# Talking-heads attention and an FFT mixer on one core: a batch's rows in seven blocks of 60 and one of 40 places

## The chip, the core and the metric

One core of a Trainium2 chip runs the whole program. The metric is the device time of one execution in microseconds; the time of a kernel is the median of its runs. A profile is of one further execution, whose own time is given beside it.

## The reference

For 8 batches, 12 heads, 448 places and 64 elements a head: scores of all heads, mixed over the heads, softmax, mixed over the heads again, times v; then an FFT over places and channels, a layer norm, and a two-layer network with a ReLU.

```python
scores = scale * np.matmul(q, k.transpose(0, 1, 3, 2))
scores = np.einsum('bhij,hg->bgij', scores, w_pre)
attn = softmax(scores)
x = matmul(np.einsum('bhij,hg->bgij', attn, w_post), v)   # to (8, 448, 768)
u = x + np.real(np.fft.fft(np.fft.fft(x, axis=1), axis=2))
un = (u - mean(u)) / np.sqrt(var(u) + 1e-06)
out = u + np.maximum(un @ w_ch1, 0.0) @ w_ch2
```

All is float32.

## The kernel before

The program has two stages. The mixing stage (`mix_phase`) makes u for each batch and stores it in DRAM; the feed-forward stage (`ffn_phase`) loads u in 512-row tiles, normalises it and multiplies by the weights with a Strassen-like scheme of seven products. The stages meet in one place: the first tiles of u are loaded when the mixing stage has given its memory back, and the last Fourier pieces of the last batch run as "parts" between the first products.

**Steps.** The mixing stage goes through places in steps of 20: a step holds five places on each of four quarters (two row blocks of PSUM's partitions z, two tiles x), each with 12 heads, 60 rows in all. A batch is 24 steps (`GS`), the stage 192 (`TOT`). For a step T:

- four gathers (`emit_gather`, line 475, on SP's queue) bring rows of scores from a block's tile Sb into Kr, so that heads lie on partitions; they are issued four steps ahead (`LG`);
- premix (`emit_premix`, line 486, PE, 8 matmuls) mixes heads, two steps (`LM`) before the step's postmix; two maxima on DVE (line 493), two exponentials on ACT (line 500), reciprocals on DVE (507, 508) and two scalings on POOL (510);
- postmix (`emit_postmix`, line 520, PE, 8 matmuls) mixes again, and DVE transposes the result into Pv (`emit_turn`, line 531).

**Blocks.** Three steps (`BS`) share a block of 60 places: `emit_qk` (line 459) computes the scores of a block in three shares of 8 matmuls, one for each pair of heads; ACT copies them to Sb (the helper at line 330). Sb has two buffers.

**Groups.** Two blocks make a group of six steps (`GT`), 112 rows of x (`GR`). A batch has four groups. When its steps are over, `emit_av` (line 547) multiplies Pv by v in three calls of 28 instructions, 120 columns wide, and ACT copies the result to XT, in an order of places that lets groups be added as mirror images: `PLACE` says where a group's two blocks go and which columns are set to zero (line 569). Neighbouring groups need a few rows twice, so 8 blocks of 60 places compute 480 places for 448 rows. `emit_x` (line 580) transposes XT into X; there are six buffers of X and one of XT.

**Fourier part.** The two X of a pair are folded on POOL (`fold`, lines 601 to 622), z is computed from them (`emit_z`, line 645), and `emit_s2` (line 661) adds the second transform into X by four DVE additions (lines 672, 674). After the second of a pair, X is stored: one X by SP (line 692), the other by an indirect DMA on POOL (line 684), and for the second pair a single row by SP (line 690).

**Order.** [...] A loop over steps s goes through one of two orders of pieces (`ORDERS`, for even and odd s). Pieces beside the steps stand in lists with a due step counted from the batch's first: `AT_T` (transpositions of q and k, line 434), `AT_L` and `AT_V` (loads on POOL's queue), `AT_QK`, `AT_AV`, `AT_X`, `AT_Z`, `AT_S`. Copies out of PSUM wait in a list `pend` until a `flush`; stores wait in `later` until the scale of a following step, folds go two to a step. The loop ends 29 steps after the first step of the last batch (`AT_X[-1]`):

```python
while s <= TOT - GS + AT_X[-1]:
    ...
return fold_rest, [lambda t, fn=fn: part(fn, t)
                   for _, _, fn in fill["full"] + [(0, 0, None)]]
```

Pieces of kind "full" that are due later are the parts. The feed-forward stage loads tiles 0 and 1 of u (line 910, SP), takes statistics (935), computes powers on POOL (940 to 943), runs the folds that are left (`fold_rest`, POOL), normalises (951) and transposes (960). In the products of the first tile (`first`, line 1026) a part is run after the first product and after the fourth to the seventh, and one after each of the second layer's (line 1099). The conversion of the weights from 64-bit floats (lines 231 to 267) goes on DVE, one operation a step, and later in the feed-forward stage.

Of the kernel before, what the change touches and what calls it, by code (L numbers as in the profile page):

```python
# [10 lines left out]
F32 = mybir.dt.float32  # L11
# [18 lines left out]
R = 5  # L30
KR = R * NH
RS = 12
NB = 56
BS = 3
GT = 2 * BS
GR = 2 * NB
NG = S // GR
GS = NG * GT
ROWS = ((0, NB), (S - GR + 1, S - NB + 1), (GR, GR + NB), (GR * 2 + 1, GR * 2 + 1 + NB))
PR = (GR, GR + 1)  # L40
PN = GR + 1


PLACE = ((0, 1, (GR,)), (GR - 1, -1, (0, GR)), (GR, -1, ()), (1, 1, (0,)))
XW = GR + 12

ENDS = (GR, GR * 2 + 1, GR * 3 + 1, S)
TOT = B * GS
# [10 lines left out]

SH = S // 2
DH = DM // 2
DQ = DH // 2
CW = DQ // 2 + 1
# [8 lines left out]

AT_T = ((6, 10), (17, 18), (14, 16))
AT_L = ((-4, -3), (-2, -1), (0, 1), (2, 8), (12, 13), (14, 15))
AT_V = ((3, 4), (5, 6), (7, 7))
AT_QK = ((1, 2, 2), (0, 1, 2), (0, 1, 2), (1, 1, 2),  # L80
         (0, 1, 2), (0, 1, 2), (0, 1, 2), (0, 1, 2))
AT_AV = ((1, 2, 3), (0, 1, 5), (3, 4, 5), (1, 2, 4))
AT_X = (11, 20, 24, 29)
AT_Z = (39, 39, 41, 41)
AT_S = ((40, 44), (48, 54))

ORDERS = tuple(o.split() for o in (
    "conv pre post flush AV max0 exp0 "
# [202 lines left out]
def mix_phase(ctx, tc, rest, ident, q, k, v, w_pre, w_post, u_scr, u_rev, wts):  # L291
# [8 lines left out]
    def pool(name, bufs=1, **kw):  # L300
        return ctx.enter_context(tc.tile_pool(name=name, bufs=bufs, **kw))

    def late(name, bufs=1):
        return rest.enter_context(tc.tile_pool(name=name, bufs=bufs, side="right"))
# [8 lines left out]
    wts.open(ctx, tc)  # L313
    pvv = pool("pvv")
    ppv = pool("ppv", 2)
    pxt = pool("pxt")
    pxx = late("pxx", 6)
    pxs = late("pxs")
    pxf = late("pxf")
    pzz = late("pzz")  # L320
# [63 lines left out]
    batches = [dict() for _ in range(B)]  # L384
    first = {}
    START = sorted(range(3), key=lambda xx: max(AT_T[xx]))
    blocks = [dict(b=n // (2 * NG), r0=ROWS[n // 2 % NG][n % 2]) for n in range(2 * NG * B)]
    groups = [dict(b=n // NG, gi=n % NG) for n in range(NG * B)]
    steps = [dict() for _ in range(TOT)]

    def emit_load_qk(b, xx, nm, y):
# [54 lines left out]
    def emit_qk(n, xx):  # L446

        bk = blocks[n]
        st = batches[bk["b"]]
        if "Sb" not in bk:  # L450
            bk["Sb"] = psb.tile([P, 6, S], F32, name="Sb", tag="Sb")
        r0 = bk["r0"]
        pss = [ms_tile() for _ in range(2)]
        for y in range(2):
            for lo in (r0 + MG * y, r0 + MG * y + 32):
                o = 64 * y + lo - r0 - MG * y
                hi = min(lo + 32, r0 + 64)
                for x in range(2):
                    nc.tensor.matmul(  # L459
                        pss[x][o:o + hi - lo, :S],  # L460
                        st["qT", xx][64 * x:64 * x + 64, y, lo:hi],
                        st["kT", xx][64 * x:64 * x + 64, y, :],
                        start=True, stop=True)
        return [lambda x=x: copy(ENG["QK"][x], bk["Sb"][:124, 2 * xx + x, :],
                                 pss[x][:124, :S]) for x in range(2)]

    def emit_gather(T):

        Kr = pkr.tile([P, 2, S], F32, name="Kr", tag="Kr")
        Sb = blocks[T // BS]["Sb"]  # L470
        row = _row(Sb)
        for z in range(2):
            for x in range(2):
                p0 = MG + 4 * (T % BS) + 2 * z + x
                nc.sync.dma_start(
                    out=Kr[64 * x:64 * x + KR, z, :],
                    in_=_ap(Sb, p0 * row, [[RS * row, 2 * R], [S, 6], [1, S]]))
        steps[T]["Kr"] = Kr

    def emit_premix(T):  # L480
# [44 lines left out]

    def emit_turn(T):

        g = groups[T // GT]
        if T % GT == 0:
            g["Pv"] = ppv.tile([P, GT, 2 * S], F32, name="Pv", tag="Pv")  # L530
        nc.vector.transpose(  # L531
            g["Pv"][:, T % GT, :].rearrange("p (z s) -> p z s", z=2),
            steps[T]["po"][:, :, :S])
        steps[T].clear()

    def emit_av(g, pr):

        st = batches[g["b"]]
        Pv = g["Pv"]
        rp = _row(Pv)  # L540
        nu = GT * 4
        pss = [ms_tile() for _ in range(2)]
        for jb in range(C7):
            for x in range(2):
                for y in range(2):
                    i = 2 * pr + x
                    nc.tensor.matmul(  # L547
                        pss[y][64 * x:64 * x + 64, :nu * R],
                        st["v", pr][64 * y:64 * y + 64, x, jb * D:(jb + 1) * D],
                        _ap(Pv, 64 * y * rp + 32 * jb + R * i,  # L550
                            [[rp, 64], [HS, nu], [1, R]]),
                        start=(jb == 0), stop=(jb == C7 - 1))
        if pr == 0:
            g["XT"] = pxt.tile([P, 6, XW], F32, name="XT", tag="XT")
        XT = g["XT"]
        rx = _row(XT)
        first, sg, none = PLACE[g["gi"]]

        def done(y):
            rs = _row(pss[y])  # L560
            for e in range(2):

                o = MG + first + sg * NB * e
                dst = _ap(XT, (3 * y + pr) * XW + o, [[rx, P], [sg * RS, R], [sg, RS]])
                src = _ap(pss[y], 60 * e, [[rs, P], [1, R], [R, RS]])
                copy(ENG["AV"][y], dst, src)
            if y == 1 and pr == 2:
                for o in none:
                    nc.vector.memset(XT[:, :, MG + o:MG + o + 1], 0.0)
        return [lambda y=y: done(y) for y in range(2)]  # L570

    def emit_x(g):
        X = pxx.tile([PN, DM], F32, name="X", tag="X")
        XT = g.pop("XT")
        g["X"] = X
        evs = []
        for u in range(2):
            ps = ms_tile()
            for i in range(3):
                nc.tensor.transpose(ps[:PN, i * P:(i + 1) * P],  # L580
                                    XT[:, 3 * u + i, MG:MG + PN], ident[:, :])
            evs.append(lambda u=u, ps=ps: copy(ENG["X"][u], X[:, u * DH:(u + 1) * DH],
                                               ps[:PN, :DH]))
        if g["gi"] % 2:
            fold(g)
        return evs

    def fold(g):
# [1 line left out]

        st = batches[g["b"]]
        pair = g["gi"] // 2
        Xa, Xb = groups[g["b"] * NG + g["gi"] - 1]["X"], g["X"]
        pl = nc.gpsimd
        box = []

# [103 lines left out]
    def due(kind, at, fn):  # L700
        fill[kind].append((at, len(fill[kind]), fn))
# [4 lines left out]
    for b in range(B):  # L706
# [23 lines left out]
        for pr in range(3 if b else 0):  # L730
            for y in range(2):
                due("none", f + AT_V[pr][y], lambda b=b, pr=pr, y=y: emit_load_v(b, pr, y))
        for n in range(0 if b else 2, 2 * NG):
            for xx in range(3):
                due("QK", f + BS * n - 7 + AT_QK[n][xx],
                    lambda n=2 * NG * b + n, xx=xx: (emit_qk(n, xx), n))
        for n in range(NG):
            g = groups[b * NG + n]
            for pr in range(3):
                due("AV", f + GT * (n + 1) + AT_AV[n][pr],  # L740
                    lambda g=g, pr=pr: (emit_av(g, pr), None))
            due("full", f + AT_X[n], lambda g=g: emit_x(g))
        for n, at in enumerate(AT_Z):
            due("full", f + at, lambda b=b, n=n: emit_z(b, n // 2, n % 2))
        for pair in range(2):
# [27 lines left out]
    s = int(min(v_[0][0] for v_ in fill.values()))  # L773
    ET = mybir.EngineType
    with tc.manual_schedule(engines={ET.PE, ET.DVE, ET.Activation, ET.Pool}):
        while s <= TOT - GS + AT_X[-1]:
            old = len(later)
            n = take("none", s)
            ahead, now = 0 <= s + LM < TOT, 0 <= s < TOT
            for op in ORDERS[s % 2]:  # L780
                if op == "flush":
                    flush()
                elif op in fill:
                    take(op, s)
                elif op == "conv":
                    if s >= 4:
                        wts.deal(1)
                elif op == "gather":
                    if 0 <= s + LG < TOT:
                        if any(e[2] is not None and e[2] <= (s + LG) // BS for e in pend):  # L790
                            flush()
                        emit_gather(s + LG)
                elif op == "scale":
                    if ahead:
                        emit_scale(s + LM)
                    for _ in range(old):
                        later.pop(0)()

                    if s < TOT - 3:
                        for _ in range(min(len(folds), 1 if n and s > 3 else 2)):  # L800
                            folds.pop(0)()
                elif op in ("post", "turn"):
                    if now:
                        (emit_postmix if op == "post" else emit_turn)(s)
                elif ahead:
                    (emit_premix if op == "pre" else emit_max if op[0] == "m"
                     else emit_exp)(s + LM, *map(int, op[3:]))
            s += 1
        flush()
        wts.deal(1000)  # L810
# [559 lines left out]
```

## Time and profile before

| | us |
|---|---|
| median of 3 runs | 2387.02 |
| lowest, highest | 2384.95, 2389.32 |
| the profiled execution | 2384.91 |
| its span | 2383.1 |
| PE busy | 2307.2 (97%) |
| DVE busy | 1739.4 (73%) |
| POOL busy | 1145.6 (48%) |
| ACT busy | 1131.5 (47%) |

The span is the stretch from the first to the last instruction in the profile; the execution's own time is 1.8 us longer. A row of the profile names a line of the code, an engine, the tiles (out<-in), and how often the instruction ran. The trace counts a float32 matmul of the small shapes twice, so that the 8 instructions of a premix are x16 there. "Kr<-Sb" is a gather, "ms" a PSUM tile of the pieces beside the steps, "mx" and "po" those of premix and postmix.

### The profile page before, as it was taken

How to read it: one execution, taken by the hardware profiler on the slowest of the kernel's cores; microseconds unless marked ns; L12 is line 12 of the kernel's file. 1: busy time of each engine (PE TensorE's matmuls, PEld its weight loads, DVE VectorE, ACT ScalarE, POOL GpSimd, SP SyncE). 2: the span in 40 equal slices, each digit the busy share in tenths (PEclk: the TensorE clock that was granted, in tenths of full speed). 3: DMA queues.
4: the chain of work that ended last, by engine and by line, in shares of the span. 5: the costliest groups of instructions: out<-in, count | busy, mean ns of one | idle time of the engine just before them, and what ended most of it. 6: DMA issues, size and time to landing. Idle time of an engine off the chain costs nothing.

```text
span 2383.1 us, 59994 instructions
## 1 busy us (share of the span) xinstructions
PE 2307.2 (97%) x22856; PEld 1740.8 (73%) x22856; DVE 1739.4 (73%) x3636; ACT 1131.5 (47%) x3101; POOL 1145.6 (48%) x1684
## 2 busy tenths in 40 slices
PE   6999999999999969999999999999999999999998
PEld 2555555555565557767777779999899999999997
DVE  3888888889887746776676767777767777776556
ACT  4777776666667522232122224444444444444444
POOL 3687877878776451211234353334333433343333
PEclk8999999999999979999999999999999999999999
DMA  7565555656554555656888795569456846674553
GB/s 169 167 175 169 183 170 159 198 163 182 174 174 156 196 161 174 222 194 228 243 246 226 209 310 127 153 174 260 126 152 179 227 133 184 166 214 118 146 127 67
DMA packets 215627, 429.07 MB, mean 180 GB/s; under 512 B 39086, under 2 KB 137670, under 8 KB 215342
## 3 DMA queue, kind: packets, MB, share of 16 engines
q1 hardware_dynamic: 144686, 283.82, 34.8%
q0 software_dynamic: 64656, 139.45, 26.8%
q8 instruction: 183, 3.00, 0.6%
q10 hardware_dynamic: 6000, 1.97, 0.5%
q14 instruction: 102, 0.84, 0.1%
HBM read 213.16 MB, written 129.39 MB: 144 GB/s over the span
## 4 chain that ended last, share of the span: by engine, by line
PE 85%; DMA 4%; DVE 4%; POOL 2%; issue 2%; ACT 1%; SPq 1%; ACTq 0%; POOLq 0%; DVEq 0%
PE psP L1026 17%; PE psP L1156 10%; PE psR L1026 9%; PE mx L486 7%; PE ms L547 6%; PE psP L1099 6%; PE ms L459 5%; PE po L520 5%; PE psR L1156 5%; PE psQ L1026 4%; PE psR L1099 3%; DMA Kr<-Sb 3%; PE psQ L1156 2%; PE ms L661 2%; PE psQ L1099 1%
## 5 line engine op out<-in xcount | busy, mean ns | idle before, releaser
L1026 PE MATMUL psP<-ub,w1t 128*128 128x256 f32 x2016 | 482.8, 380 | 0.2 <-DVE h L1045 0.2
L1026 PEld LDWEIGHTS psP<-ub,w1t 128*128 128x128 f32 x2016 | 380.7, 191 | 49.1 <-DVE h L1045 0.6
L510 POOL TENSOR_SCALAR PP<-PP,rcp 128x448 f32<-128x448 f32 x384 | 254.7, 672 | 220.6 <-DVE rcp L508 190.2
L500 ACT ACTIVATE PP<-mx,nmx 128x448 f32<-128x448 f32 x384 | 240.7, 632 | 167.4 <-DVE nmx L493 153.5
L493 DVE TENSOR_REDUCE nmx<-mx 128x1 f32<-128x448 f32 x384 | 222.6, 617 | 91.0 <-PE mx L486 89.5
L1190 POOL DMA_DIRECT2D out_dram<-od x109 | 133.1, 1405 | 280.8 <-DVE od L1187 147.6
L486 PE MATMUL mx<-Kr,kw 60*32 60x448 f32 x3072 | 233.8, 549 | 15.9 <-DMA Kr<-Sb 12.2
L990 POOL TENSOR_TENSOR hq<-h 128x256 f32<-128x256 f32 (+1 forms) x168 | 104.3, 621 | 293.4 <-ACT h L1046 173.2
L1026 PE MATMUL psR<-ub,w1t 128*128 128x256 f32 x1008 | 231.3, 379 | 0.0
L1187 DVE TENSOR_TENSOR od<-od 128x768 f32<-128x768 f32 x196 | 188.6, 974 | 52.4 <-ACT od L1184 50.6
L531 DVE STREAM_TRANSPOSE Pv<-po 128x896 f32<-128x896 f32 x192 | 212.6, 1107 | 10.4 <-PE po L520 7.3
L520 PE MATMUL po<-PP,kw 60*32 60x448 f32 x3072 | 212.3, 537 | 2.7 <-POOL PP L510 1.8
L459 PE MATMUL ms<-kT,qT 64*32 64x448 f32 (+1 forms) x3072 | 205.6, 544 | 7.2 <-ACT qT L330 6.3
L1026 PEld LDWEIGHTS psR<-ub,w1t 128*128 128x128 f32 x1008 | 191.4, 190 | 25.9
L330 ACT COPY Sb<-ms 124x448 f32<-124x448 f32 x384 | 184.0, 542 | 33.0 <-DMA Kr<-Sb 15.1
L547 PEld LDWEIGHTS ms<-Pv,vv 64*64 64x64 f32 x5376 | 143.1, 132 | 70.9 <-issue 36.0
L1184 ACT COPY od<-psP 128x192 f32<-128x192 f32 x390 | 125.0, 320 | 145.6 <-PE psP L1156 141.4
L213 POOL DMA_DIRECT2D raw<-in_moe_w_ch_dram x88 | 53.0, 603 | 261.9 <-DVE tmp L257 255.1
L547 PE MATMUL ms<-Pv,vv 64*64 64x120 f32 x5376 | 166.7, 267 | 1.1 <-issue 1.1
L1099 PE MATMUL psP<-w2t,h 128*128 128x384 f32 x448 | 153.7, 486 | 0.0
L1045 DVE TENSOR_TENSOR h<-h,psP 128x512 f32<-128x512 f32 x42 | 28.8, 687 | 148.9 <-PE psP L1026 148.7
L459 PEld LDWEIGHTS ms<-kT,qT 64*32 64x32 f32 (+1 forms) x3072 | 67.9, 106 | 79.9 <-issue 51.8
(141 smaller groups left out, 4602.1 us busy)
## 6 DMA issues: line engine op xcount, KB each, us to landing
ub<-ub SPq DMA_DIRECT2D x294, 384.0 KB
Kr<-Sb SPq DMA_DIRECT2D x768, 105.0 KB
out_dram<-od POOLq DMA_DIRECT2D x137, 384.0 KB, 6.1
w1t<-w SPq DMA_DIRECT2D x42, 384.0 KB
w2t<-w SPq DMA_DIRECT2D x42, 384.0 KB
raw<-in_moe_w_ch_dram POOLq DMA_DIRECT2D x56, 256.0 KB, 5.2
raw<-in_moe_w_ch_dram POOLq DMA_DIRECT2D x32, 384.0 KB, 4.0
w<-wst POOLq DMA_DIRECT2D x92, 128.0 KB, 3.9
```

Of the source, the lines that this page charges most:

```text
L459: nc.tensor.matmul(pss[x][o:o + hi - lo, :S], st["qT", xx][64 * x:64 * x + 64, y, lo:hi], st["kT", xx][64 * x:64 * x + 64, y, :], start=Tr ...
L486: nc.tensor.matmul(mx[x][64 * z + o:64 * z + o + 32, :S], kw1[64 * x:64 * x + KR, o:o + 32], Kr[64 * x:64 * x + KR, z, :], start=True, sto ...
L493: nc.vector.tensor_reduce(nmx[:, :], steps[T]["mx"][x][:, :S], axis=AX.X, op=ALU.max, negate=True)
L500: nc.scalar.activation(steps[T]["PP"][:, x, :], steps[T]["mx"][x][:, :S], ACTF.Exp, bias=steps[T]["nmx", x][:, :], accum_out=steps[T]["den ...
L510: nc.gpsimd.tensor_scalar(PP[:, x, :], PP[:, x, :], rcp[:, x:x + 1], 1.0, op0=ALU.mult, op1=ALU.mult)
L520: nc.tensor.matmul(po[o:o + 32, z, :S], kw2[64 * z:64 * z + KR, y, :], PP[64 * z:64 * z + KR, :, c * HS:(c + 1) * HS], start=True, stop=True)
L531: nc.vector.transpose(g["Pv"][:, T % GT, :].rearrange("p (z s) -> p z s", z=2), steps[T]["po"][:, :, :S])
L547: nc.tensor.matmul(pss[y][64 * x:64 * x + 64, :nu * R], st["v", pr][64 * y:64 * y + 64, x, jb * D:(jb + 1) * D], _ap(Pv, 64 * y * rp + 32 ...
L1026: nc.tensor.matmul(p[:, m, :], w1[i][:, kc, m * P:(m + 1) * P], ub[:, kc, :], start=i in (0, 4, 1)[:3 - seed] and m == kc == 0, stop=kc == ...
L1099: nc.tensor.matmul(p, h[:, LHS[i], kf, x * P:(x + 1) * P], w2[i][:, kf, :], start=i in (0, 4, 1)[:3 - (c > 0)] and kf == 0, stop=kf == FM ...
L1156: nc.tensor.matmul(ps[j, key][:, :DQ], a, b, start=m in (0, 4), stop=True, skip_group_check=True)
L1187: eng.tensor_tensor(D[j][:, :, :], D[j][:, :, :], D[k][:, :, :], op=ALU.add)
```

## The change

A batch has 23 steps. Its 448 rows lie in eight blocks, seven of 60 places and one of 40 (`BLOCKS`: first place, places of a fifth, steps, group, first column, direction). Blocks lie without overlap in the two halves of the batch; the block of 40 has two steps, so that the third and fourth blocks make five steps (`GROUP_AT`), and the width of the products with v is 120 or 100 columns. Two blocks no longer make one group's rows exactly: a block that straddles two groups is written to one XT, and the columns that belong to the other are copied over on POOL (`SPILL`). For this XT has two buffers, and X five. Since the second group of a pair can be ready before the first, `emit_x` runs in the order 0, 1, 3, 2 (`AT_X`), and the rows are folded when groups 1 and 2 are done. Due steps move: those after the middle of a batch by one, `AT_X` and the second pair of `AT_S` by more. The loop ends 30 steps after the last batch's first.

```diff
-RS = 12
-NB = 56
-BS = 3
-GT = 2 * BS
-GR = 2 * NB
-NG = S // GR
-GS = NG * GT
-ROWS = ((0, NB), (S - GR + 1, S - NB + 1), (GR, GR + NB), (GR * 2 + 1, GR * 2 + 1 + NB))
+RS = 12
+SH = S // 2
+GR = SH // 2
+NG = 4
+BLOCKS = ((0, RS, 3, 0, 0, 1), (60, RS, 3, 0, 60, 1),
+          (412, 8, 2, 1, 36, -1), (352, RS, 3, 1, 96, -1),
+          (292, RS, 3, 3, 68, 1), (232, RS, 3, 3, 8, 1),
+          (172, RS, 3, 2, 52, -1), (112, RS, 3, 2, 112, -1))
+NBL = len(BLOCKS)
+BLOCK_AT = [sum(k[2] for k in BLOCKS[:n]) for n in range(NBL + 1)]
+GS = BLOCK_AT[-1]
+GROUP_AT = BLOCK_AT[::2]
+GT = 6
+SPILL = {2: (3, 113, 15, 1, 111), 3: (2, -1, 7, 3, 1)}
+NONE = {0: (0, (GR,)), 2: (1, (0, GR)), 3: (3, (0,))}
...
-AT_T = ((6, 10), (17, 18), (14, 16))
-AT_L = ((-4, -3), (-2, -1), (0, 1), (2, 8), (12, 13), (14, 15))
+AT_T = ((5, 9), (16, 17), (13, 15))
+AT_L = ((-4, -3), (-2, -1), (0, 1), (2, 7), (11, 12), (13, 14))
...
-AT_X = (11, 20, 24, 29)
+AT_X = ((11, 0), (23, 1), (28, 3), (30, 2))
 AT_Z = (39, 39, 41, 41)
-AT_S = ((40, 44), (48, 54))
+AT_S = ((40, 44), (46, 50))
...
-    pxt = pool("pxt")
-    pxx = late("pxx", 6)
+    pxt = pool("pxt", 2)
+    pxx = late("pxx", 5)
...
-        nu = GT * 4
+        nu = (GROUP_AT[k + 1] - GROUP_AT[k]) * 4
...
             if y == 1 and pr == 2:
-                for o in none:
-                    nc.vector.memset(XT[:, :, MG + o:MG + o + 1], 0.0)
+                if k in SPILL:
+                    gi, c0, n, go, co = SPILL[k]
+                    Xo = groups[b * NG + go]["XT"]
+                    back = -1 if gi == 2 else 1
+                    nc.gpsimd.tensor_copy(
+                        out=_ap(Xo, PG[go] + co, [[rx, P], [XW, 6], [1 - 2 * (go == 1), n]]),
+                        in_=_ap(XT, PG[gi] + c0, [[rx, P], [XW, 6], [back, n]]))
+                if k in NONE:
+                    gi, cols = NONE[k]
+                    for o in cols:
+                        Xo = groups[b * NG + gi]["XT"]
+                        nc.vector.memset(Xo[:, :, PG[gi] + o:PG[gi] + o + 1], 0.0)
...
-                due("QK", f + BS * n - 7 + AT_QK[n][xx],
-                    lambda n=2 * NG * b + n, xx=xx: (emit_qk(n, xx), n))
+                due("QK", f + BLOCK_AT[n] - 7 + AT_QK[n][xx],
+                    lambda n=NBL * b + n, xx=xx: (emit_qk(n, xx), n))
...
-        while s <= TOT - GS + AT_X[-1]:
+        while s <= TOT - GS + AT_X[-1][0]:
```

What a step, a QK share, a T, X, z or S piece does is as before; the block of 40 gives 104 rows of scores in place of 124.

## The prediction

> **What bounds the kernel now.** I read the page first (shares, clock and slices), then the chain of waits in two stretches (300 to 360 us, inside the mixing stage, and 822 to 892 us, where it hands over to the feed-forward stage), then the timelines of DVE and PE there. The mixing stage is 192 steps; its last transposition (line 531) starts at 828.3 us. The page has PE busy 97% of the span, but ends of matmuls are modelled, so I take PE's prices from the chain:
>
> ```profile
> 308.28 0.91 PE mx L486 x16
> 309.19 0.75 PE po L520 x16
> 309.94 1.50 PE ms L459 x32
> ...
> 313.81 1.49 PE ms L661 x8
> 315.30 0.66 PE ms L580 x6
> ...
> 323.94 6.39 DMA Kr<-Sb
> ...
> 340.79 1.64 PE ms L547 x56
> ```
>
> Columns are start, length, piece. PE runs back to back: premix 0.9, postmix 0.75, one share of QK (x16) 0.75, one product with v ("AV") 1.65, a second-transform piece S 1.5, a transposition of XT ("X") 0.75. The same chain gives 0.8 for a q/k transposition (T) and 1.73 for two z pieces. What interrupts PE is a late gather (Kr<-Sb). Few steps of before are without an extra piece, so whether a step may be shorter than its PE work lets it be is seen only in batch 0. DVE there, start and length ahead of the line:
>
> ```profile
> 59.64 1.14 DVE L493 TENSOR_REDUCE nmx<-mx 128x1 f32<-128x448 f32 x2
> 60.85 1.12 DVE L531 STREAM_TRANSPOSE Pv<-po 128x896 f32<-128x896 f32 x1
> ...
> 62.44 0.29 DVE L243 TENSOR_SCALAR wst<-tmp 128x256 uint32<-128x256 uint32 x1
> 62.65 1.15 DVE L493 TENSOR_REDUCE nmx<-mx 128x1 f32<-128x448 f32 x2
> ```
>
> This step holds premix, postmix and one QK alone: 2.4 us of PE work, yet 3.0 us pass from one pair of maxima to the next, with DVE full. So a bare step costs 3.1 (3.15, 3.01 and 3.24 in batch 0), not 2.4. A step with S costs at least 4.86 (both such steps of batch 7 without T), since its four additions of 0.55 come on top of DVE's work. The seam between the stages:
>
> ```profile
> 832.04 4.88 PE ms L547 x153
> ...
> 837.01 4.45 DMA u<-u
> 841.48 0.30 SPq L910
> 841.83 8.37 DMA u<-v
> ...
> 876.13 1.01 POOL xf L622
> 877.18 1.44 PE ms L645 x6
> ```
>
> The rows u can be loaded only when the last AV has freed their memory; the statistics follow, then POOL's folds (line 601 to 622, 854.8 to 877.2), and the first z piece (line 645) waits for the folds. PE meanwhile does this:
>
> ```profile
> 863.91 1.47 PE L661 MATMUL ms<-tcs,z 96*113 96x193 f32 x8
> ...
> 865.22 2.75 PE L1026 MATMUL psR<-ub,w1t 128*128 128x256 f32 x12
> ...
> 867.81 2.75 PE L1026 MATMUL psP<-ub,w1t 128*128 128x256 f32 x12
> ...
> 870.40 2.75 PE L1026 MATMUL psQ<-ub,w1t 128*128 128x256 f32 x12
> ```
>
> From 878 us on the chain is PE almost alone to the end of the kernel: PE work that is pushed behind 878 us lengthens the kernel by its own length.
>
> [...] So what stands behind a waiting z piece waits too; the trace agrees (nothing of line 1026 starts between 873.1 and 876.2). [...] The trace shows a granted clock of 0.53 to 0.61 in 840 to 860 us, and a group of line 1026 that takes 4.94 at 878.6 us in place of 2.59. [...] SP's and POOL's transfers share the 16 engines; in 840 to 850 us these are busy 1.02 of the time at 260 GB/s. [...]
>
> **The change, part by part.**
> 1. A step per batch goes (8 in all): eight premix and eight postmix matmuls, two maxima, two exponentials, a transposition, two scalings, four gathers. One AV of each batch's four groups (3 of 12 calls) has 100 columns in place of 120: 1.65 x 100/120 = 1.38; bounds 1.38 and 1.65. QK stays (24 shares a batch). PE's sum for a batch is now 24 x 1.65 + 24 x 0.75 + 12 x 1.65 + six T 4.8 + four X 3.0 + z 3.46 + four S 6.0 = 94.7; after, 92.2. PE alone gives 2.5 us a batch.
> 2. But the other pieces are spread anew. By the order of PE's instructions, a middle batch before has ten steps of AV+QK (4.05 each), one AV alone (3.3), two QK+QK (3.15), two QK+X (3.15), three QK+T (3.2), two S+X (4.86), two S+T (5.33, measured), z 4.13, AV+z+T 5.2 (measured): 95.7. After: AV+QK 4 x 4.05, with 100 columns 3.78, AV+QK+S 2 x 5.55, S+X 4.86, QK+QK+AV 4.8, five bare steps 5 x 3.1, QK+X+T 3.95, AV+QK+X 4.8, AV+QK+T 4.85, the same with X and 100 columns 4.53, QK+T 2 x 3.2, AV+z+T 4.95, S+T 5.33, QK+QK+z 4.88: 95.9 for 23 steps. Five bare steps lose 0.7 each, which eats the gain: +0.2 a batch, +1 for six middle batches. Batch 0 (no S and no z; all its first steps sit at 3.1) comes out 2.3 shorter, the last batch 1.2 shorter. Together -2.5.
> 3. Measured, batches 1 to 6 take 101.6 each (transposition at 131.8 to that at 741.3), 5.9 over my 95.7: mostly waits for Kr. I leave them as they are, since the loads that crowd the gathers stay; bounds -3 and +2 a batch.
> 4. 23 is odd, so every second batch runs with the two orders of a step swapped. The sum does not see it: 0, bounds -1 and +2 for such a batch.
> 5. X has five buffers, XT two. In even batches the X of the next batch's second group takes the buffer whose store is issued one step before. In the trace such a store (line 692) is issued at 319.8, for an S that began at 313.7; a landing of the other store (line 684) took 5.1. That is 11.2 against three steps, 12.6: hidden by 1.4 us. If the cover goes, ACT waits with the exponentials behind it: up to 3 us in four batches. I take 0.
> 6. Added: two copies of spilled rows a batch on POOL (90 and 42 elements; between 0.18 of line 616 and 0.6 of line 615). They run in POOL's wait for DVE's reciprocals (129 us idle from 100 to 800 us); X's transpositions wait for them, a step later in most cases. 0; uncovered 0.5 each, 8 us. Copies of 40 in place of 60 elements are under ACT's other work: 0. Weight conversion (160 DVE operations, one a step) still ends inside the stage.
> 7. The seam. S of batch 6's second pair, due at 54 before, fell past the loop and was the first part run inside the feed-forward stage (863.91 above). Now due at 50, it runs in the loop's tail right behind the last AV. Two things follow. (a) Its SP store (336 KB) and a single row stand in SP's queue between the first loads of u; they wait for DVE's last addition, 3.6 us after S begins (829.8 to 833.4 in the trace for such a piece), with the other u loads behind them. Its indirect store stands on POOL's queue ahead of the weight loads; nobody needs those soon. 672 KB at 260 GB/s is 2.6 us of shared engines. Loads of u land 0 to 5.8 later; I take 3.5. (b) The parts move up by one: the first z piece now stands where S stood, ahead of the three groups of line 1026. PE blocks at it until the folds are done, and 3 x 2.59 = 7.8 us move behind 876 us. S itself saves nothing, it lay in PE's wait. Bounds 5 and 10 [...]. Seam: +11.3.
>
> Sum: -2.5 + 11.3 = +8.8. Against the profiled execution, 2384.91 (span 2383.1), that is 2393.7; the median of the runs shown is 2.1 higher, so about 2395.
>
> **Rivals.**
> - PE is the bound on the mean, and the room in bare steps coincides with waits for Kr: speaks for it that the chain in 300 to 360 us is PE and Kr waits only; against it the DVE rows above. Each batch then gains the 2.5 of PE: -19.7 + 11.3 = -8.4, 2379. It decides for faster once a middle batch drops below about 99.5.
> - The seam is absorbed (POOL's folds finish early, or DMA has room): -2.5 alone, 2384, no change. Against it: the folds depend on u's loads as before.
> - The swapped orders and 5.5 us steps beside bare ones make gathers late more often, or X's buffer is waited for: +2 a batch more, +16, 2411. For it: gathers are issued two steps ahead, and four of them occupy SP 3.1 us, as long as a bare step.
> That the change does not do what it says is excluded: premix stands in PE's order 184 times in place of 192.
>
> **How the numbers follow.** Forecast 0.47 (alone 2389 to 2402), PE-bound 0.2, absorbed seam 0.1, more waits 0.23. Some 0.2% is what a measurement can tell from no change: below 2382.2 is faster, above 2391.8 slower. Faster 0.18 (most of the first rival), same 0.2 (the second, and the forecast's low edge), slower 0.62. The range, 2377 to 2412, leaves out a part of the first and third rival.
>
> **What would show it.** Right: middle batches between 99.5 and 103.5 us; bare steps near 3.1; line 645's first wait some 12 us with line 1026 behind it; the time from the last AV to the first z up by some 3 us. Wrong: bare steps near 2.5, waits for Kr halved or doubled, ACT's copy to X waiting for a DMA, or no long wait at line 645.

## The result, and the profile after it

The kernel became slower: 2423.98 us median (2420.56 to 2426.66, 6 runs) against 2385.94 (2379.56 to 2389.32, 6 runs), ratio 1.0161 (95% interval 1.0145 to 1.0177; below, intervals stand in brackets). That is +38 us where +8.8 was forecast: slower, as forecast, but above the range of 2377 to 2412. The profiled execution took 2420.56 us, the fastest of the six.

PE's busy time and the shares of the chain that ended last, from the page of the kernel before:

```profile
PE 2307.2 (97%) x22856; PEld 1740.8 (73%) x22856; DVE 1739.4 (73%) x3636; ACT 1131.5 (47%) x3101; POOL 1145.6 (48%) x1684
...
PE 85%; DMA 4%; DVE 4%; POOL 2%; issue 2%; ACT 1%; SPq 1%; ACTq 0%; POOLq 0%; DVEq 0%
```

and of the kernel after:

```profile
PE 2307.4 (95%) x22600; PEld 1726.4 (71%) x22600; DVE 1706.3 (71%) x3596; ACT 1106.3 (46%) x3069; POOL 1133.5 (47%) x1684
...
PE 73%; issue 7%; DVE 6%; POOL 6%; DMA 4%; ACT 3%; SPq 1%; ACTq 0%; POOLq 0%; DVEq 0%
```

The instructions have gone as planned (PE 22856 to 22600), and no engine is busier by more than 0.2 us. But PE's share of the chain fell from 85% to 73%: the lost time is spent in waits of one engine for another. A few marks in both traces say where:

| us from the span's start | before | after | grown by |
|---|---|---|---|
| last transposition of the mixing stage | 828.3 | 853.5 | 25.2 |
| end of the last AV | 836.9 | 861.2 | 24.3 |
| first transposition of un | 856.0 | 884.0 | +3.7 more |
| first second-layer product | 891.5 | 927.0 | +7.5 more |
| span | 2383.1 | 2418.7 | nothing more |

So the mixing stage, expected 2.5 shorter, is some 25 longer; the rest is the seam, 3.7 and 7.5, together 11.2 against 11.3 forecast. From transposition to transposition, batches 1 to 6 took 101.6 us each before and 105.2 after.

**The seam.** PE's timeline after, 884 to 912 us (start, length; in brackets the idle time ahead and what ended it):

```profile
889.68 2.76 PE L1058 MATMUL psP<-ub,w1t 128*128 128x256 f32 x12
...
904.36 0.69 PE L677 MATMUL ms<-ts,xf 113*97 113x113 f32 x2 [11.92 <-POOL xf L654]
...
906.54 3.98 PE L1058 MATMUL psR<-ub,w1t 128*128 128x256 f32 x12
```

One product, then the first z piece, which waits 11.9 us (its weight load 12.3) for POOL's last fold, with the next product behind it. This is the picture that was forecast. Ahead of it, in the chain of waits after, the single row's store (SPq L722) waits for the landing of the indirect store (v<-X,rows), and the loads of u stand behind it:

```profile
864.27 7.77 DMA v<-X,rows
...
872.06 0.22 SPq L722
...
872.33 3.07 DMA u<-v
```

**The mixing stage.** The waits between 100 and 800 us (engine, line and what it waited for: us in all, times, longest; PEld is PE's weight load, PE the matmul), before:

```profile
ACT PP L500 <- DVE nmx L493: 124.9, 136, 2.9
...
PEld mx L486 <- DMA Kr<-Sb: 23.1, 32, 2.8
...
PEld mx L486 <- ACT PP L500: 13.6, 41, 1.1
...
PE mx L486 <- ACT PP L500: 2.0, 3, 0.9
```

and after:

```profile
ACT PP L518 <- DVE nmx L511: 172.6, 149, 4.6
...
PEld mx L504 <- ACT PP L518: 55.6, 83, 3.5
...
PEld ms L612 <- POOL XT L594: 18.1, 10, 3.5
...
PEld mx L504 <- DMA Kr<-Sb: 11.5, 21, 2.0
...
PE ms L612 <- POOL XT L594: 11.1, 10, 2.7
...
PE mx L504 <- ACT PP L518: 10.2, 15, 2.6
```

PE's waits for gathers (Kr) have halved. Two others have grown. Premix waits longer for exponentials on ACT: its weight loads 55.6 us where they waited 13.6, its matmuls 10.2 where they waited 2.0. And X's transpositions wait ten times for the copy of spilled rows on POOL, a wait that did not exist: 18.1 us by their weight loads, 11.1 by their matmuls. The two rows of a pair must not be added. They show the same waits: at 156.3 us both end, after 3.5 us for the weight load and 2.7 for the matmul. The weight load's wait begins earlier, while the matmuls ahead of it are still at work; what PE lost by the trace is the matmul's. These two waits are what the experiments take apart.

How the first comes about, in the timeline of all engines after, 499 to 511.5 us:

```profile
502.12 1.16 DVE L511 TENSOR_REDUCE nmx<-mx 128x1 f32<-128x448 f32 x2 [1.09 <-PE mx L504]
...
504.42 0.98 PE L504 MATMUL mx<-Kr,kw 60*32 60x448 f32 x16
...
504.87 0.54 DVE L269 SCALAR_TENSOR_TENSOR tmp<-raw,tmp 128x384 f32<-128x384 uint32 x1
...
505.32 1.13 DVE L342 COPY qT<-ms 128x512 f32<-128x512 f32 x1
...
506.26 1.89 DVE L273 TENSOR_TENSOR wst<-wst,tmp 128x384 f32<-128x384 f32 x1
...
508.08 1.14 DVE L511 TENSOR_REDUCE nmx<-mx 128x1 f32<-128x448 f32 x2
508.78 0.63 ACT L518 ACTIVATE PP<-mx,nmx 128x448 f32<-128x448 f32 x1 [2.96 <-DVE nmx L511]
...
509.56 0.18 PEld L504 LDWEIGHTS mx<-Kr,kw 60*32 60x32 f32 x8 [3.45 <-ACT PP L518]
```

The step up to 502 has an AV: PE is busy with it, and DVE idles 1.09 us before its maxima. Then come three steps with little for PE, a T, nothing, a T. Now DVE is full, busy 5.93 of the 5.96 us from 502.12 to 508.08: besides its own work it copies qT (1.13) and converts (0.54 and 1.89). The next maxima are 6 us behind the last, ACT's exponential waits 2.96 us for them, and the premix that needs the PSUM tile of that exponential waits 3.45. PE's matmuls are idle for 2.65 us ahead of 509.56, and no AV or S piece of another step starts in this time: those stand elsewhere in PE's order. The longest of its kind, this wait is one of 37 above 0.8 us in the stage; whether such waits carry the 25 us is for the experiments.

The second wait, in the chain of waits after, 338 to 392 us:

```profile
338.14 1.03 POOL v L716
339.17 0.36 POOL rawq L422
339.53 0.51 issue
340.04 0.71 POOL rawq L422
340.75 0.28 POOL XT L594
341.07 0.91 PE ms L612 x6
```

The copy itself takes 0.28 us. Ahead of it in POOL's queue stand the issues of an indirect store and of two loads, 2.6 us in all. The rows that it copies stood in XT from 336.5 us, when ACT's last copy there ended; it starts at 340.7, when the last of these issues ends. The issues held POOL for 0.71 to 1.03 us each, which is more than the 0.28 us copy behind them.

### The profile page after: what moved, and what is told of

It reads as the page before. It is cut to its first block, busy times and chain, and to the rows that moved or that the text cites. A ratio compares the mean times of both kernels' runs of the same rounds, so it can differ in the third digit from the quotient of the medians.

```text
span 2418.7 us, 59291 instructions
## 1 busy us (share of the span) xinstructions
PE 2307.4 (95%) x22600; PEld 1726.4 (71%) x22600; DVE 1706.3 (71%) x3596; ACT 1106.3 (46%) x3069; POOL 1133.5 (47%) x1684
## 4 chain that ended last, share of the span: by engine, by line
PE 73%; issue 7%; DVE 6%; POOL 6%; DMA 4%; ACT 3%; SPq 1%; ACTq 0%; POOLq 0%; DVEq 0%
PE psP L1058 15%; PE psP L1188 10%; PE psR L1058 8%; PE mx L504 5%; PE psR L1188 5%; PE ms L568 5%; PE psQ L1058 4%; PE psP L1131 4%; PE ms L476 4%; PE po L538 4%; PE psQ L1188 2%; DMA Kr<-Sb 2%; PE psR L1131 2%; PE ms L693 2%; ACT PP L518 1%
## 5 line engine op out<-in xcount | busy, mean ns | idle before, releaser
L1058 PEld LDWEIGHTS psP<-ub,w1t 128*128 128x128 f32 x2016 | 379.0, 190 | 49.5 <-DVE h L1077 1.6
L528 POOL TENSOR_SCALAR PP<-PP,rcp 128x448 f32<-128x448 f32 x368 | 239.3, 659 | 255.7 <-DVE rcp L526 218.6
L518 ACT ACTIVATE PP<-mx,nmx 128x448 f32<-128x448 f32 x368 | 230.6, 631 | 217.9 <-DVE nmx L511 203.8
L511 DVE TENSOR_REDUCE nmx<-mx 128x1 f32<-128x448 f32 x368 | 215.2, 618 | 104.0 <-PE mx L504 101.5
L476 PE MATMUL ms<-kT,qT 64*32 64x448 f32 (+2 forms) x3072 | 208.5, 544 | 8.3 <-ACT qT L342 6.3
L551 DVE STREAM_TRANSPOSE Pv<-po 128x896 f32<-128x896 f32 x184 | 203.9, 1108 | 9.9 <-PE po L538 7.8
L342 ACT COPY Sb<-ms 124x448 f32<-124x448 f32 (+1 forms) x384 | 184.5, 540 | 27.8 <-PE ms L476 22.6
L568 PE MATMUL ms<-Pv,vv 64*64 64x120 f32 (+1 forms) x5376 | 161.7, 263 | 0.8 <-issue 0.6
L504 PEld LDWEIGHTS mx<-Kr,kw 60*32 60x32 f32 x2944 | 48.1, 106 | 124.1 <-ACT PP L518 74.3
```

Source lines behind the costliest of these rows:

```text
L476: nc.tensor.matmul(pss[x][o:o + hi - lo, :S], st["qT", xx][64 * x:64 * x + 64, y, lo:hi], st["kT", xx][64 * x:64 * x + 64, y, :], start=Tr ...
L504: nc.tensor.matmul(mx[x][64 * z + o:64 * z + o + 32, :S], kw1[64 * x:64 * x + KR, o:o + 32], Kr[64 * x:64 * x + KR, z, :], start=True, sto ...
L511: nc.vector.tensor_reduce(nmx[:, :], steps[T]["mx"][x][:, :S], axis=AX.X, op=ALU.max, negate=True)
L518: nc.scalar.activation(steps[T]["PP"][:, x, :], steps[T]["mx"][x][:, :S], ACTF.Exp, bias=steps[T]["nmx", x][:, :], accum_out=steps[T]["den ...
L528: nc.gpsimd.tensor_scalar(PP[:, x, :], PP[:, x, :], rcp[:, x:x + 1], 1.0, op0=ALU.mult, op1=ALU.mult)
L551: nc.vector.transpose(turned[a]["Pv"][:, j, :].rearrange("p (z s) -> p z s", z=2), steps[T]["po"][:, :, :S])
```

## The experiments

Edits are to the kernel after, unless before is named; ratios are to the kernel before. "Waits" are PE's from 100 to 800 us, each of one profiled execution.

### The spill copy alone: spill_act, spill_dve

```diff
-                    nc.gpsimd.tensor_copy(
+                    nc.scalar.copy(
```

> The changed kernel with its two copies of spilled rows on ACT in place of POOL; nothing else. Theory A (X's transpositions wait on PE for the POOL copy, which stands behind DMA issues on POOL's queue: ten waits of 1.0 to 3.5 us between 100 and 800 us): these waits shrink to the 0.7 us that PE also waits for ACT elsewhere, 1.0 to 1.5 us are won at each of 14 places, 15 to 22 us in all, about 2404. Theory B (the loss is that premix, QK and fill are spread unevenly over 23 steps, so that steps of 5.5 to 6.5 us stand beside bare ones): the waits only change their name, within 5 us of the changed kernel, 2419 to 2426.

Measured: 2417.87 us (4 runs), ratio 1.0137 [1.0117, 1.0156].

With `nc.vector.tensor_copy(` in the same place:

> The same two copies on DVE. Theory A: as on ACT or a little worse, since DVE's queue has the maxima and X's additions ahead of the copy: 2404 to 2412. Theory B: 2419 to 2426, or slower, since DVE is full in bare steps.

Measured: 2425.44 us (4 runs), 1.016 [1.0135, 1.0185].

With the copy on ACT the ten waits for POOL are gone from the trace, but the median is only 0.24% (6 us) lower, with intervals that overlap, just below theory B's range and far from theory A's 2404, and with the copy on DVE not lower at all. In the profiled run of spill_act, the longest of its four (that of after is the shortest of its six), batches 1 to 6 are no shorter (98.9 to 109.6 us): premix's waits grew in exchange, for exponentials from 55.6 to 59.8 us, for gathers from 11.5 to 17.9 (weight loads alone). So the copy's wait is worth some 6 of the 38 us, or nothing, while the other one stands.

### The order at the seam: part_gap, part_gap_actq

```diff
-                       for _, _, fn in fill["full"] + [(0, 0, None)]]
+                       for _, _, fn in [(0, 0, list)] + fill["full"] + [(0, 0, None)]]
```

An empty part stands where the S piece stood before, so that z moves back behind three products.

> The changed kernel with an empty part ahead of the others, so that the first z piece stands behind the fourth product of the first tile again, as before the change. If 7.8 us of products were pushed behind the folds: 7 to 8 us faster than the changed kernel, about 2416.5, and the wait at the first z piece falls from some 12 us to some 4. If the seam's loss is that the rows u come later: no change, within 2 us.

Measured: 2418.63 us (4 runs), 1.0146 [1.0124, 1.0169]. PE's timeline of this run, 880 to 912 us:

```profile
896.02 2.75 PE L1058 MATMUL psP<-ub,w1t 128*128 128x256 f32 x12
898.62 2.75 PE L1058 MATMUL psR<-ub,w1t 128*128 128x256 f32 x12
901.21 2.75 PE L1058 MATMUL psP<-ub,w1t 128*128 128x256 f32 x12
903.80 2.75 PE L1058 MATMUL psQ<-ub,w1t 128*128 128x256 f32 x12
910.72 0.43 PE L677 MATMUL ms<-ts,xf 113*97 113x113 f32 x2 [4.17 <-POOL xf L654]
```

Behind the first product three more groups again run before the z piece, which now waits 4.2 us in place of 11.9 (its weight load 4.6 in place of 12.3); un to second layer takes 34.2 us in place of 43.0 (before: 35.5). That is 8.8 us in the trace. The medians alone show less, 5.4 us with intervals that overlap; the pair spread_act and spread_act_gap below measures it better.

Further, the two stores of that pair go to ACT's queue, out of the way of the loads of u:

```diff
+            eng = nc.scalar if b == B - 2 and pair else nc.sync
...
-                        nc.sync.dma_start(out=u_rev[b][GR:GR + 1, :], in_=X[GR:GR + 1, :])
+                        eng.dma_start(out=u_rev[b][GR:GR + 1, :], in_=X[GR:GR + 1, :])
...
-                    nc.sync.dma_start(
+                    eng.dma_start(
```

> As with the empty part, and the last stores of the last batch but one (one of 336 KB and one row) are issued by ACT in place of SP, so that the loads of u do not stand behind them. If standing behind them costs the 2.8 us by which normalisation starts late after the last transposition: about 2 to 3 us faster than with the empty part alone, 2414. If it is their bytes on the shared DMA engines: no change against the empty part alone.

Measured: 2421.53 us (4 runs), 1.0154 [1.0137, 1.0172]; from the last AV to the first transposition of un 21.8 us, against 21.7 in part_gap. The row's store no longer holds the loads of u, but other transfers then stand in the chain (w2t<-w for 8.5 us, u<-u for 6.4), and nothing is won. The stretch is 19.1 to 22.0 us (mean 20.3) in four traces of the kernel before and its variants, 21.3 to 22.9 (mean 22.0) in thirteen of after and its variants. The means differ by some 1.8, so how much of the +3.7 belongs to the change stays open.

### The due steps: spread

Only due steps change, so that every step of a middle batch holds at least two pieces beside its own work: no bare step, with one QK share alone, is left (five a batch in after) and no AV+QK+S.

```diff
-AT_T = ((5, 9), (16, 17), (13, 15))
+AT_T = ((5, 10), (16, 17), (13, 15))
...
-AT_QK = ((1, 2, 2), (0, 1, 2), (0, 1, 2), (1, 1, 2),
+AT_QK = ((0, 2, 1), (0, 1, 2), (0, 1, 2), (1, 2, 2),
...
-AT_AV = ((1, 2, 3), (0, 1, 5), (3, 4, 5), (1, 2, 4))
-AT_X = ((11, 0), (23, 1), (28, 3), (30, 2))
+AT_AV = ((1, 2, 3), (0, 1, 3), (3, 4, 5), (1, 2, 4))
+AT_X = ((10, 0), (23, 1), (28, 3), (29, 2))
...
-AT_S = ((40, 44), (46, 50))
+AT_S = ((40, 42), (46, 49))
```

> The changed kernel with its pieces beside the steps spread again, by due steps alone: no step is left with one QK share only, no step holds S beside a product with v, the largest sum of pieces in a step falls from 4.2 to 3.3 us of PE work. All instructions are the same. Theory B (uneven spread: in bare steps PE waits for the exponentials, 5.5 us a batch against 0.6 before the change): a batch falls from 105.2 to 98 to 102 us, 25 to 50 us in all, 2375 to 2400. Theory C (the chain of maximum and exponential and DVE's sum of work pace every step, however the pieces lie): within 6 us of the changed kernel, 2418 to 2430.

Measured: 2404.85 us (4 runs), 1.0082 [1.0056, 1.0107]: half of the loss is gone, and the time lies between the two theories. Batches 1 to 6 take 103.0 us each, 105.2 in after. Its waits:

```profile
PEld ms L612 <- POOL XT L594: 22.7, 8, 4.3
...
PEld mx L504 <- DMA Kr<-Sb: 21.1, 23, 3.5
...
PE ms L612 <- POOL XT L594: 16.3, 7, 3.5
PEld mx L504 <- ACT PP L518: 14.7, 38, 1.6
```

The weight loads of premix wait 14.7 us for exponentials again, where the kernel before had 13.6. The wait for POOL's copy is now among the largest (22.7 us by weight loads, 16.3 by matmuls): a T and the first X of a batch's second pair share a step, and in even batches that step takes 9.1 us.

### Is it the row store? row_late, b_row_late

A rival for the stage: the store of a single row stands in SP's queue ahead of gathers (in the chain of waits after, gathers are issued behind it at 370.6 us). It is moved one step later, in after and, the same edit, in before.

```diff
-                        nc.sync.dma_start(out=u_rev[b][GR:GR + 1, :], in_=X[GR:GR + 1, :])
+                        later.append(lambda X=X: nc.sync.dma_start(
+                            out=u_rev[b][GR:GR + 1, :], in_=X[GR:GR + 1, :]))
```

> The changed kernel with the single row's store (one per batch) a step later in SP's queue. Where it stands now it waits for the indirect store's landing, 3.6 us in the trace, with gathers behind it. If this is what makes the gathers late after the second pair's S: 1 to 3 us a batch, 8 to 24 us faster than the changed kernel, 2400 to 2416. If the gathers are late for the loads that crowd the DMA engines: within 4 us of it.

Measured: 2424.25 us (4 runs), 1.0171 [1.0139, 1.0204].

> The kernel before with the same single edit. If the row's store makes its gathers late (30 us of waits for Kr on PE from 100 to 800 us): 8 to 20 us faster than before, 2364 to 2376. If the loads do: within 4 us of before.

Measured: 2386.75 us (20 runs), 1.0000 [0.9989, 1.0012]. No effect in either that the intervals show; this rival falls.

### Taking the parts together: spread_gap_row, spread_act, spread_act_gap

spread_gap_row is spread with the empty part and the late row store.

> The changed kernel with the pieces spread, the empty part in the seam and the row's store a step later. If the three add: 7 to 8 us below the spread one for the seam, and what the row's edit alone gives: 2350 to 2390; below the kernel before only if spreading brings a batch under some 100 us.

Measured: 2393.12 us (20 runs), 1.0029 [1.0016, 1.0042], 11.7 us below spread, more than the 7 to 8 expected, of which un to second layer gives 8.7 in the traces (34.5 us, 43.2 in spread). The other two are spread with the copy on ACT, without and with the empty part.

> The spread kernel with the spilled rows copied by ACT in place of POOL. Theory D (the waits behind POOL's copy, 39 us between 100 and 800 us in the spread kernel, are real time once no bare step follows that would have been as long anyhow): 12 to 30 us faster than the spread kernel, 2375 to 2393. Theory E (they only hide other waits, as in the unspread kernel, where ACT in place of POOL left the batches as long): within 4 us of it, 2401 to 2409.

Measured: 2398.19 us (20 runs), 1.0036 [1.0023, 1.0048]. The waits for the copy are gone, and the ratio falls by 0.46% against spread, 11 us with wide intervals. The pair spread_gap_row and spread_act_gap below, 20 runs each, gives 0.25%, 6 us; it differs also in the row's store, which had no effect above. With even steps the copy's queue place does cost, 6 to 11 us, between the two theories. Theory D's 39 us count each wait twice, by its weight load and by its matmul; PE's matmuls waited 16.3. Part of it returns as other waits, in the waits of spread_act:

```profile
PEld mx L504 <- DMA Kr<-Sb: 28.4, 31, 4.3
...
PEld mx L504 <- ACT PP L518: 20.9, 41, 2.4
```

> The same with the empty part in the seam: 7 to 9 us below the one without it; theory D: 2367 to 2386, theory E: 2393 to 2402.

Measured: 2390.32 us (20 runs), 1.0004 [0.999, 1.0017]. Against spread_act 7.9 us: the z piece's place, which the forecast had at 7.8. In all the time lies between theories D and E. The kernel with the shorter batch now equals before, no more.

### Two more due steps: spread_t6, spread_t6_l8

To spread_act_gap, first the transposition that shared a step with X goes one step later, then two loads on POOL's queue move together:

```diff
-AT_T = ((5, 10), (16, 17), (13, 15))
+AT_T = ((6, 10), (16, 17), (13, 15))
...
-AT_L = ((-4, -3), (-2, -1), (0, 1), (2, 7), (11, 12), (13, 14))
+AT_L = ((-4, -3), (-2, -1), (0, 1), (8, 9), (11, 12), (13, 14))
```

> The same with one transposition of q a step later, out of the step that holds the third group's X (9 us in every second batch). If that step is long for its own sum of work: 1 to 3 us a batch, 8 to 20 us below the one before it. If it is long for the wait behind POOL's copy alone, which is gone: no change, within 4 us.

Measured: 2386.03 us (20 runs), 0.9992 [0.9979, 1.0004], 4.3 us below spread_act_gap with intervals that overlap: it decides for neither reading.

> The same with one load of q or k at the steps 8 and 9 in place of 2 and 7, away from the loads of v (steps 3 to 7) and the stores of X. If bursts of loads make the gathers late in the two or three steps after: waits for Kr on PE fall from some 28 to under 20 us, and 5 to 12 us are won. If they are late for SP's issue or other reasons: no change, within 4 us.

Measured: 2381.45 us (17 runs), 0.9972 [0.9957, 0.9987]: faster than both kernels, than before by 0.3%, and the best of several variants tried. Against spread_t6 the intervals overlap. The expected fall of the waits for gathers did not come (by weight loads 24.4 us in spread_t6); the waits of this run:

```profile
PEld mx L504 <- DMA Kr<-Sb: 23.5, 30, 3.5
...
PEld mx L504 <- ACT PP L518: 16.8, 43, 1.2
```

So whether the loads' place helps, and why, is open.

### The same cause in the kernel before: b_uneven

If unevenness is the cause, it must cost in the 24-step kernel too. Three pieces of before move so that three steps a batch become bare; the instructions stay the same.

```diff
-AT_T = ((6, 10), (17, 18), (14, 16))
+AT_T = ((6, 9), (17, 18), (15, 16))
...
-AT_X = (11, 20, 24, 29)
+AT_X = (11, 20, 24, 28)
```

> The kernel before, 24 steps, with three pieces moved by their due steps alone (two transpositions of q and k and one of XT), so that three steps of each batch hold one QK share only and three others hold a piece more. All instructions are the same. Theory B (bare steps cost some 3.1 us whatever PE has to do): 0.7 to 1.0 us for each of three steps in seven batches, 14 to 22 us slower than before. If the changed kernel's loss came of its copies, widths or buffers alone: within 4 us of before.

Measured: 2395.99 us (4 runs), 1.0055 [1.0034, 1.0075], and the wait for exponentials again (before: 13.6):

```profile
PEld mx L486 <- ACT PP L500: 32.2, 67, 1.3
PEld mx L486 <- DMA Kr<-Sb: 26.3, 30, 2.8
```

Less than expected, but the effect stands in a kernel that has neither the copy nor the shorter batch. The lengths of its steps in the two profiled runs, from maxima to maxima in batches 1 to 6, suggest how. The three steps that lost a piece got 0.4 us shorter together (3.48, 3.10 and 3.63 before; 3.89, 2.74 and 3.16 now), the three that took one 2.2 longer (14.1 to 16.3). A piece taken out of a light step saved little, and put elsewhere it cost nearly its price.

### Is DVE's sum the floor? conv2, b_conv2

The conversion of the weights deals two operations a step in place of one, so that it ends halfway through the stage and later batches run without it. In after, then in before:

```diff
-                        wts.deal(1)
+                        wts.deal(2)
```

> The changed kernel with two operations of the weight conversion on DVE a step in place of one, so that it ends in the fourth batch and batches 4 to 6 have none. If DVE's sum of work sets the bare steps' length: these batches get 2 to 5 us shorter than the 106.7 us of the same batches of the changed kernel, and bare steps fall from 3.1 to 2.6. If the chain of maximum and exponential sets it: no change, within 1 us a batch.

Measured, one run: 2433.61 us. Batches 0 to 6 take 94.9, 108.4, 113.8, 113.5, 103.1, 101.8 and 102.6 us.

> The same edit on the kernel before. Its steps are filled with PE work, so batches 4 to 6 should change little under either theory, by at most 1.5 us from 102.3 us.

Measured, one run: 2396.82 us; batches 94.5, 105.7, 110.1, 105.7, 99.2, 100.0 and 97.7 us.

Batches 4 to 6 gain 4.2 us each in after (106.7 to 102.5) and 3.3 in before (102.3 to 99.0), where before was expected to gain little. Batches 1 to 3, with twice the conversion, get longer, by 7.0 to 10.2 us in after and 3.3 to 9.5 in before. In after, the bare steps of these batches fall from 3.2 to 2.6 us on the mean, as expected if DVE's sum sets their length, while the long ones stay (AV+QK+S 6.7 and 6.9, AV+QK+T 6.7 and 6.5). What leaves these batches lightens DVE, but its loads and stores leave too, so the runs do not tell DVE from DMA. As far as one run of each can show it, the conversion is not what makes after slower than before: without it the gap is still 3.5 us a batch (4.4 with it).

## Why the prediction was wrong

The direction came out right through the seam; for the mixing stage alone the forecast had the wrong sign (2.5 shorter, measured some 25 longer).

**Step 2, the table of step lengths, failed.** It priced a step at the sum of its PE pieces, or 3.1 if bare (steps with S as measured), and gave +0.2 a batch; measured +3.6. Mean lengths in batches 1 to 6, from maxima to maxima:

| step (after) | price | measured |
|---|---|---|
| five bare | 3.1 each | 3.24, 3.00, 2.92, 3.20, 3.00 |
| AV+QK+S, two | 5.55 | 6.36, 6.49 |
| AV+QK+T | 4.85 | 6.32 |
| QK+X+T | 3.95 | 5.42 |
| QK+QK+AV | 4.8 | 5.41 |
| AV+QK+X | 4.8 | 5.36 |
| QK+T, two | 3.2 | 4.20, 4.01 |

The bare price was right on the mean, though it is no floor: a bare step took 2.5 in some batches, 3.5 to 4.2 in others. Steps with AV+QK alone kept to their price too (3.98 for 4.00 on the mean of five, one of them with 100 columns). What was mis-sized is the steps with three pieces, and those with QK+T: the eight steps of the lower rows exceed their prices by 7.7 us a batch, of which 1.1 in QK+X+T is PE's wait for POOL's copy. Not all of this is loss, since a long step can shorten its neighbour: the first AV+QK+S is followed by an AV+QK of 3.33, and the two take 9.69 for 9.60. Firm is the sum over a batch. In all, after exceeds its table by 9.3 (105.2 for 95.9), before by 5.9, and 9.3 - 5.9 + 0.2 is the 3.6. Before's excess lay in other steps, half of it in the ten of AV+QK (4.35 for 4.05); carried over as a constant, it said nothing of the new steps. The kernel before has no bare step after its first batch, and no step with QK, AV and a third piece: it showed nothing of how DVE and PE fare when long steps and light ones follow each other, and the pieces' sums were carried over from even steps. spread (-0.79%, due steps alone) shows that the distribution costs some 19 us, and b_uneven (+0.55%) that uneven steps cost without the rest of the change. What in the distribution costs, the bare steps or the pieces that meet in the long ones, is not separated: spread changes both.

**Step 3** left the waits for gathers as they were. They halved (23.1 to 11.5 by weight loads), and came back, 21.1 and more, as soon as the steps were even; that PE simply came later for other reasons in between fits this, and is not shown. Of loads that crowd the gathers the trace before has this much: the DMA engines are busy 0.90 of the time in 320 to 325 us, where the gather of 6.39 us begins, and 0.29 in 305 to 315. That this makes gathers late is shown by no run (spread_t6_l8 moved two loads, and the waits by weight loads went from 24.4 to 23.5 us). Waits moved from one cause to another in nearly every run.

**Step 6 failed in its reason.** "They run in POOL's wait for DVE's reciprocals" looked at POOL's idle time on the whole; what counted was what stands ahead in its queue at that place, 2.6 us of issues at 338 us. X's transpositions waited up to 2.7 us (their weight loads 3.5) for a 0.28 us copy. The "uncovered" price, 8 us, is near what it cost once the steps were even (6 to 11), but by luck: it priced 0.5 us for each copy itself, and what cost was the queue ahead. Beside the uneven steps it shows less (spill_act, some 6 or nothing); that the two waits cover each other there is a reading.

**Steps 1, 4 and 5 were right.** A product with 100 columns got shorter as priced (1.22 us from its first matmul's start to its last one's, 1.45 with 120). Odd and even batches are alike on the mean (105.4 and 104.9), though single steps are not. No copy of ACT to X waited for a DMA before the last AV; two in the seam did (1.5 us at 863.3, 7.2 at 871.4), ahead of folds that begin only at 882.9.

**Step 7 was right in size**, 11.2 for 11.3: (b) 7.5 in the trace and 7.9 in the medians for 7.8, by the mechanism described; (a) 3.7 for 3.5, in part by luck. The row's store did hold the loads of u, but for the landing of the indirect store (7.8 us in the chain), not for DVE's last addition; taking both stores out of SP's queue changed nothing, and on the mean of all traces the stretch grew by some 1.8 only. That SP's and POOL's transfers share the engines shows in 840 to 850 us of before: SP's queue took 61.7% of the 16 engines' time and POOL's 40.1%, together the 1.02 of the prediction. The bound of 10 for (b) was the author's estimate. (The sum from the median, 2387.02 + 8.8, is 2396, not 2395.)

**Batch 0 and the last batch**, expected 2.3 and 1.2 shorter, took 0.5 and 2.4 longer; they have bare and long steps too; what they lost was not taken apart.

**The rivals.** PE was not the bound on the mean, and the seam was not absorbed. More waits, at +2 a batch, was nearest in size, and it named the long steps beside bare ones; but the waits that it saw coming from them, late gathers and X's buffer, are not the ones found.

The sum by runs, in parts of 38 us: uneven steps about 19, the copy behind POOL's issues 6 to 11, the z piece 8, the rest within the intervals. With all three undone (spread_act_gap) the change is worth nothing, although PE has 2.5 us less to do a batch. In that trace the batches 1 to 6 take 102.5 us, 0.9 more than before, so that 3.4 us a batch are to be explained. The waits of premix's matmuls for gathers and exponentials grew from 8.3 to 19.3 us in 100 to 800 us, 1.6 us for each of 6.8 batches (by weight loads from 36.7 to 49.5, 1.9 a batch): about half. The other half is not found. What keeps gathers and exponentials at the old pace, whether their own length, DVE's or the DMA engines' load, is not settled; conv2 and b_conv2 only show that batches get shorter in both kernels when conversion and its transfers are gone.

## What to carry to other kernels

Where engines are coupled step by step through small buffers, as here, the time is a sum of step lengths, and PE's work alone does not set every one of them: a bare step took 2.9 to 3.2 us on the mean for 2.4 us of PE's work. Taking a step out and piling its pieces on others can cost more than the step: here a batch had 2.5 us less for PE to do and took 3.6 us more. So give every step something, and price a combination only by a step that the trace holds. An operation placed on an idle engine can cost what stands ahead of it in that engine's queue, DMA issues included: here 2.6 us of issues ahead of a 0.28 us copy. A wait that goes away is not yet time won; other waits can take its place: in spill_act ten waits for POOL, 18.1 us by weight loads, went, and the median fell by 6 us, with intervals that overlap. Where a piece is taken from a list whose order is the order of the engine, look at what moves up into its place: here it was a z piece that waits 11.9 us for POOL with the next product behind it, and it cost 7.9 us by the medians.

## What the runs showed of the hardware that was not expected

A copy of 90 elements on 128 partitions takes 0.27 us on POOL (340.74 us in after) and 0.27 on ACT (331.00 us in spread_act): its own length was not the issue, the place was. The issue of one plain load held POOL for 0.71 us, longer than that copy. Executions of one kernel scatter by more than most of the effects sought: spread_act ran from 2387.92 to 2401.82 us, and the waits of one trace move from gathers to exponentials and back between variants. A reading of a few microseconds from a single trace needs the medians beside it.
